# Local attention in four-bank units with the band mask multiplied in by VectorE, and the last head pair of each global attention normalized through TensorE and ScalarE

## The chip, the cores and the metric

The kernel runs on one core of one Trainium2 chip. The metric is the device time of one execution in microseconds (us). Engine names are those of the profile: PE is TensorE (PEld its weight loads), DVE is VectorE, ACT is ScalarE, POOL is GpSimd, and SP issues transfers. Each engine works through its own list of instructions; the order in that list is fixed when the kernel is built, partly by the order in which the program emits them and partly by a scheduler that moves them.

## The reference, cut to what matters

```python
x = A_x                                             # (1, 2048, 512) bf16, 32 heads of 16
x = x + _A_ref(_layernorm(x), A_wqkv, A_wo)         # local: each query sees 8 keys, 0, 2, ... 14 back
x = x + _B_ref(_layernorm(x), B_wq, B_wk, B_wv, B_wo)   # global: 2048 keys, one shared K and V head
x = x + _A_ref(_layernorm(x), A_wqkv, A_wo)
x = x + _B_ref(_layernorm(x), B_wq, B_wk, B_wv, B_wo)
```

So four stages run one after the other, A0, B0, A1 and B1. A later stage needs the whole result of the one before, with a LayerNorm between.

## The kernel before

The sequence is cut into four chunks `c` of 512 rows (even and odd positions lie in different chunks, so a dilated window of 8 becomes a dense band). A chunk is projected (`a_in`), attended (`a_attn`), projected out (`a_out`), and its LayerNorm and projections for the B stage follow (`b_in`). `a_attn` goes over four head groups `t` of 8 heads; the texts call one such `t` a head pair. The part that the argument touches:

```python
for t in range(4):                                 # a_attn(c), before
    o, dn = ...                                    # two PSUM banks: outputs, softmax sums
    for gh in range(2):
        for kd in range(2):                        # a unit: two row groups, two PSUM banks
            st = self.sps.tile([128, 2, 512], F32, name="s")            # sps has 2 buffers
            for j in range(2):                     # band mask (0 or -30000) added by PE
                nc.tensor.matmul(st[:, j, 0:ncol], lhsT=self.w.ident[:], rhs=self.w.band[:, 0:ncol],
                                 start=True, stop=False)
            ...                                    # 8 score matmuls on top of the mask
            nc.scalar.activation(out=P[:, :, 0:ncol], in_=st[:, :, 0:ncol], func=AF.Exp, scale=DH ** -0.5)
            ...                                    # 16 PV matmuls into o, 4 sum matmuls into dn
    nc.scalar.activation(out=logs[:], in_=dn[:], func=AF.Ln)
    nc.scalar.activation(out=rec[:], in_=logs[:], func=AF.Exp, scale=-1.0)     # 1 / sums
    nc.vector.tensor_tensor(out=onc[:, t, :], in0=o[:], in1=rec[:], op=ALU.mult)
    self.checks.see_logs(logs[:], tmp[:])          # a guard: POOL adds up logs*logs
...
def run(self, plan0):                              # order of a whole A stage
    self.a_in(0, plan0)
    self.a_in(1, plan)
    for c in range(4):
        self.a_attn(c)
        if c + 2 < 4:
            self.a_in(c + 2, plan)
        self.a_out(c)
        self.b_in(c, plan)
```

In `a_in` the keys were copied out of PSUM and then masked twice by POOL. At the end of B, the last head pair was normalized like every other: its sums went by DMA to a reciprocal, on to DRAM and back as a broadcast, and only then could the last output projection run.

Of the kernel before, what the change touches and what calls it, by code (L numbers as in the profile page):

```python
# [428 lines left out]
class Checks:  # L429
# [7 lines left out]
    def __init__(self, nc, pool):  # L437
        self.nc, self.pool = nc, pool
        self.a = pool.tile([128, 512], F32, name="chk_a")
        self.b = pool.tile([128, 2, 32], F32, name="chk_b")  # L440
        nc.gpsimd.memset(self.a[:], 0.0)
        nc.gpsimd.memset(self.b[:], 0.0)

    def see_logs(self, logs, tmp):

        self.nc.gpsimd.tensor_tensor(out=tmp, in0=logs, in1=logs, op=ALU.mult)  # L446
        self.nc.gpsimd.tensor_tensor(out=self.a[:], in0=self.a[:], in1=tmp, op=ALU.add)
# [6 lines left out]
    def flag(self, psum_pool):  # L454
        nc, pool = self.nc, self.pool
        ok = pool.tile([128, 512 + 64], F32, name="chk_ok")
        for out, in_, lim in ((ok[:, 0:512], self.a[:], self.LOG_A ** 2), (ok[:, 512:544], self.b[:, 0, :], self.SUM_B),
                              (ok[:, 544:576], self.b[:, 1, :], self.REC_B)):
            nc.vector.tensor_scalar(out=out, in0=in_, scalar1=lim, scalar2=None, op0=ALU.is_lt)
        mn = pool.tile([128, 1], F32, name="chk_mn")  # L460
        nc.vector.tensor_reduce(out=mn[:], in_=ok[:], axis=AX.X, op=ALU.min)
        mb = pool.tile([128, 2], BF16, name="chk_mb")
        nc.vector.tensor_copy(out=mb[:, 0:1], in_=mn[:])
        nc.vector.memset(mb[:, 1:2], 1.0)
        cnt = psum_pool.tile([1, 1], F32, name="chk_cnt")
        nc.tensor.matmul(cnt[:], lhsT=mb[:, 0:1], rhs=mb[:, 1:2], start=True, stop=True)
        bad = pool.tile([1, 1], mybir.dt.int32, name="chk_bad")
        nc.vector.tensor_scalar(out=bad[:], in0=cnt[:], scalar1=127.5, scalar2=None, op0=ALU.is_lt)
        return bad
# [50 lines left out]
def build_band_mask(nc, cpool):  # L520
# [3 lines left out]
    nc.gpsimd.memset(m[:], 0.0)  # L524
    for h in range(2):
        for n in range(5):
            w = NQ if n < 4 else SPILL
            ap = m[64 * h:64 * h + 64, n * NQ:n * NQ + w]
            b = 0 if n < 4 else 64
            nc.gpsimd.affine_select(out=ap, in_=ap, compare_op=ALU.is_ge, fill=-30000.0, base=b, pattern=[[1, w]],  # L530
                                    channel_multiplier=-1)
            nc.gpsimd.affine_select(out=ap, in_=ap, compare_op=ALU.is_ge, fill=-30000.0, base=7 - b,  # L532
                                    pattern=[[-1, w]], channel_multiplier=1)
    return m
# [12 lines left out]
class Phase:  # L547
# [3 lines left out]
    def __init__(self, ctx, tc, x_sb, x_bf, w, QT, KAB, VE, checks, tag):  # L551
# [5 lines left out]
        self.sps = pool("As", 2, space=PSUM)  # L557
        self.ops = pool("Ao", 1, space=PSUM)
        self.mps = pool("Am", 2, space=PSUM)
        self.sm = pool("Asm", 2)  # L560
        self.xnp = pool("Axn", 4)
        self.xtp = pool("Axt", 2)
        self.qp = pool("Aq", 2)
        self.kp = pool("Ak", 3)
        self.ktp = pool("Akt", 3)
        self.pp = pool("Ap", 4)
        self.oncp = pool("Aonc", 2)
        self.np = pool("An", 2)
        self.checks = checks
        vp = pool("Av", 1)  # L570
        self.vbuf = [vp.tile([128, 8, 4, 2, 2, 32], BF16, name=f"V{i}") for i in range(3)]
        self.nhalf = vp.tile([128, 4], F32, name="nhalf")
        nc.gpsimd.memset(self.nhalf[:], -0.5)
# [3 lines left out]
        self.n = 0  # L577

    def copy(self, out, in_, act=None):

        if act is None:
            self.n += 1
            act = self.n % 2 == 0
        if act:
# [3 lines left out]
    def ln_T(self, src, plan):  # L588
# [6 lines left out]
        for i in range(4):  # L595
            nc.vector.bn_stats(out=stats[:, i, :], in_=src(i))
            nc.vector.bn_aggr(out=mv[:, i, :], in_=stats[:, i, :])
        nc.vector.tensor_scalar_add(out=ve[:], in0=mv[:, :, 1], scalar1=EPS)
        nc.gpsimd.tensor_tensor(out=rstd[:], in0=ve[:], in1=self.nhalf[:], op=ALU.pow)
# [24 lines left out]
    def a_in(self, c, plan):  # L624
# [6 lines left out]
        for t in range(4):  # L631
# [3 lines left out]
            kt_ = self.ktp.tile([128, 512], BF16, name="kt")  # L635
            self.copy(kt_[:], ps[:])
            for a in range(2):
                nc.gpsimd.tensor_scalar(out=k[:, t, :, a, :], in0=kt_[:].rearrange("p (b i) -> p b i", i=64), scalar1=self.w.kmask[:, a:a + 1], scalar2=None,  # L638
                                        op0=ALU.mult)
        v = self.vbuf[c % 3]  # L640
        wv = w_sb[:, :, 2 * D:].rearrange("p k (r a d) -> p k a r d", a=2, d=DH)
        for k2 in range(4):
# [8 lines left out]
            for gh in range(2):  # L651
                dst = v[:, 2 * k2:2 * k2 + 2, :, gh, :, 16 * gh:16 * gh + DH].rearrange("p b t j d -> p (b t) j d")
                self.copy(dst, ps[:].rearrange("p b (t h j) d -> p (b t) h j d", h=2, j=2)[:, :, gh, :, :])

    def a_attn(self, c):
# [4 lines left out]
        for t in range(4):  # L660
# [9 lines left out]
            for gh in range(2):  # L670
                for kd in range(2):
                    spill = kd == 0 and c % 2 == 1
                    ncol = 4 * NQ + (SPILL if spill else 0)
                    parts = []
                    for i in range(4):
                        kb = 4 * kd + i
                        parts.append((i * NQ, NQ if kb < 7 else 64, k, v, kb, 64 * kb))
                    if spill:
                        parts.append((4 * NQ, SPILL, kprev, vprev, 7, 0))
                    st = self.sps.tile([128, 2, 512], F32, name="s")  # L680
                    for j in range(2):
                        nc.tensor.matmul(st[:, j, 0:ncol], lhsT=self.w.ident[:], rhs=self.w.band[:, 0:ncol],  # L682
                                         start=True, stop=False)
                    for n, (col, w, kk, vv, kb, q0) in enumerate(parts):
                        for j in range(2):
                            g = 2 * gh + j
                            gs = slice(32 * g, 32 * g + 32)
                            nc.tensor.matmul(st[:, j, col:col + w], lhsT=kk[gs, t, kb, :, :],  # L688
                                             rhs=q[gs, t, q0:q0 + w], start=False, stop=(n == len(parts) - 1),
                                             tile_position=(32 * g, 0))  # L690
                    P = self.pp.tile([128, 2, 4 * NQ + SPILL], BF16, name="P")
                    nc.scalar.activation(out=P[:, :, 0:ncol], in_=st[:, :, 0:ncol], func=AF.Exp, scale=DH ** -0.5)  # L692
                    for n, (col, w, kk, vv, kb, q0) in enumerate(parts):
                        for j in range(2):
                            for a in range(2):
                                r = 2 * j + a
                                nc.tensor.matmul(o[32 * r:32 * r + 32, q0:q0 + w],
                                                 lhsT=vv[64 * a:64 * a + 64, kb, t, gh, j, :],
                                                 rhs=P[64 * a:64 * a + 64, j, col:col + w], start=first("o", r),
                                                 stop=False, skip_group_check=True, tile_position=(64 * a, 32 * r))  # L700
                    for j in range(2):
                        js = slice(64 * j, 64 * j + 64)
                        nxt = 4 if kd == 0 else 3
                        pj = P[:, j, 0:4 * NQ].rearrange("p (b q) -> p b q", q=NQ)
                        dj = dn[js, :].rearrange("p (b q) -> p b q", q=64)
                        jobs = [(dj[:, 4 * kd:4 * kd + 4, :], pj[:, :, 0:64]),
                                (dj[:, 4 * kd + 1:4 * kd + 1 + nxt, 0:SPILL], pj[:, 0:nxt, 64:NQ])]
                        if spill:
                            jobs.append((dj[:, 0, 0:SPILL], P[:, j, 4 * NQ:4 * NQ + SPILL]))
                        for out, rhs in jobs:  # L710
                            nc.tensor.matmul(out, lhsT=self.w.halves[:, gh, :], rhs=rhs, start=first("d", j), stop=False,  # L711
                                             skip_group_check=True, tile_position=(0, 64 * j))
            logs = self.np.tile([128, 512], F32, name="logs")
            rec = self.np.tile([128, 512], F32, name="rec")
            tmp = self.np.tile([128, 512], F32, name="tmp")
# [3 lines left out]
            self.checks.see_logs(logs[:], tmp[:])  # L719

    def a_out(self, c):
        nc = self.nc
        onc = self.onc.pop(c)
        for qi in range(4):
# [6 lines left out]
            nc.vector.tensor_tensor(out=self.x_sb[:, tt, :], in0=old[:, tt, :], in1=y[:], op=ALU.add)  # L731

    def b_in(self, c, plan):
# [14 lines left out]
        cols = self.VE[:, 4 * c:4 * c + 4, :, :]  # L748
        nc.gpsimd.memset(cols[:, :, :, 17:32], 0.0)
        for j in range(NJ):  # L750
            nc.gpsimd.memset(cols[:, :, j, 16:17], J_W[j])
# [6 lines left out]
    def run(self, plan0):  # L758
        plan = ("g", "a", "g", "v")
        self.a_in(0, plan0)  # L760
        self.a_in(1, plan)
        for c in range(4):
            self.a_attn(c)
            if c + 2 < 4:
                self.a_in(c + 2, plan)
            self.a_out(c)
            self.b_in(c, plan)


def attn_B_fast(ctx, tc, QT, KAB, VE, wo_sb, x_sb, S, tag, checks, out_view=None, st_bufs=2, pv_lag=3, y_gap=2,  # L770
# [8 lines left out]
    opp = ctx.enter_context(tc.tile_pool(name=f"Bf_o_{tag}", bufs=1, space=PSUM))  # L779
# [314 lines left out]
```

## Time and profile before

| | before |
|---|---|
| time, median of 3 runs | 1860.32 us (1856.23 to 1863.41) |
| span of the profiled run | 1853.3 us |
| first B exponential of B0 | 209.3 us |
| last exponential of B0 to first of B1 (joint and A1) | 229.5 us |
| last exponential of B1 to the end | 30.5 us |

I cut the span where the stages change: first transpose of A, last PV matmul of A, first and last exponential of B. The first fence is the table of busy time by stretches for the kernel before. The columns are: stretch, its length, then busy microseconds (and instruction count) of PE, PEld, DVE, ACT and POOL, then the granted PE clock as a share of full speed, the DMA share and GB/s. The lines are A0's attention, A0's tail, B0, the joint, A1's attention, A1's tail, and the end.

```profile
13.60:187.30 173.70, 158.91 (x2677) 93.03 (x2697) 68.05 (x152) 90.08 (x162) 100.02 (x80) 0.96 0.04 10
187.30:209.30 22.00, 13.40 (x85) 5.99 (x79) 9.87 (x21) 5.11 (x10) 5.13 (x5) 0.77 0.00 0
209.30:900.60 691.30, 565.83 (x5628) 190.45 (x5642) 668.87 (x1079) 687.42 (x513) 31.34 (x45) 0.99 0.05 11
900.60:934.00 33.40, 9.70 (x62) 3.29 (x60) 21.44 (x45) 3.05 (x4) 5.41 (x26) 0.71 0.05 13
934.00:1107.00 173.00, 158.39 (x2672) 92.32 (x2694) 65.30 (x137) 89.96 (x162) 99.01 (x79) 0.95 0.01 2
1107.00:1130.10 23.10, 14.57 (x85) 6.17 (x86) 10.30 (x22) 5.10 (x10) 5.12 (x5) 0.63 0.00 1
...
1822.80:1853.30 30.50, 9.82 (x58) 3.28 (x55) 8.76 (x17) 2.16 (x2) 1.77 (x3) 0.67 0.12 34
```

The B stage is bound by ACT (687 of 691 us). In A's attention PE is busy 159 of 174 us while DVE and ACT stand at 68 and 90. The change rests on the conclusion that PE bounds the stage, and that work moved from PE to DVE is won. The joint and the end are gaps in which every engine is mostly idle.

The next fence shows the groups of instructions of A that the change touches, from the page of the kernel before. A line gives the source line, the engine, the operation, the names, the shapes and the count; then busy us and the mean ns of one; then the idle time before and what ended it.

```profile
L692 ACT ACTIVATE P<-s 128x576 bf16<-128x576 f32 (+1 forms) x128 | 78.9, 650 | 50.4 <-PE s L688 50.2
L638 POOL TENSOR_SCALAR k<-kt,kmask 128x512 bf16<-128x512 bf16 x64 | 99.0, 1566 | 6.0 <-ACT kt L585 6.0
L682 PE MATMUL s<-bandmask,ident 128*128 128x288 bf16 (+1 forms) x256 | 58.5, 297 | 7.4 <-POOL bandmask L532 5.8
L711 PE MATMUL dn<-P,halves 128*64 128x256 bf16 (+3 forms) x576 | 44.7, 232 | 9.5 <-ACT P L692 9.5
```

The mask costs 58.5 us of PE over both stages, and ACT waits 50 us for scores.

The joint before, from the timeline of 899 to 938 us (start, duration, engine, line, operation, names; in brackets the idle time before it and what ended it):

```profile
906.45 0.68 DVE L854 COPY X_13953<-o_ps 128x512 f32<-128x512 f32 x1
...
914.21 3.63 SPq L510 DMA_DIRECT2D lb<-rd  x8
...
919.39 1.26 POOL L512 TENSOR_TENSOR onc<-X,lb 128x512 bf16<-128x512 f32 x1 [7.60 <-DMA lb<-rd]
...
925.86 0.69 DVE L879 TENSOR_TENSOR x_sb<-x_sb,dv 128x512 f32<-128x512 f32 x1 [0.41 <-PE dv L868]
...
926.93 1.76 DVE L575 MEMSET V_14061<- 128x2048 uint32 x1 [0.38 <-issue]
...
937.08 1.46 PE L621 MATMUL ps<-xnT,w_sb 128*128 128x512 bf16 x3 [0.82 <-DVE xnT L586]
```

Thirteen microseconds pass between the copy of the last sums and their use, nearly all of it in chained transfers, and three memsets of 1.76 us then stand ahead of the LayerNorm.

### The profile page before, as it was taken

The numbers are of one execution on the slowest core, as the hardware profiler recorded it, in microseconds if no ns is written. First come the engines' busy times: TensorE is split into PE (matmuls) and PEld (weight loads), VectorE is DVE, ScalarE is ACT, GpSimd is POOL, SyncE is SP. The second block draws the span as 40 slices with busy tenths as digits, with TensorE's granted clock in tenths as the row PEclk, the third lists the DMA queues.
The fourth block names the chain that finished last, engine by engine and source line by source line (L and its number), as shares of the span: only waits on it lengthen the run. The fifth ranks groups of instructions, "written<-read, shape, count | busy, mean of one in ns | idle before, by whom it ended". The sixth has DMA issues, their size and how long they took to land. (4 is left out here: it accounts for less than half of the span.)

```text
span 1853.3 us, 41000 instructions
## 1 busy us (share of the span) xinstructions
PE 1493.1 (81%) x16864; PEld 586.6 (32%) x16929; DVE 1533.1 (83%) x2568; ACT 1573.2 (85%) x1371; POOL 285.9 (15%) x354
## 2 busy tenths in 40 slices
PE   6998777778877888888589987777888788878884
PEld 4554222222222222222145542222222222222221
DVE  5432599999999999999744336999999999999995
ACT  3555599999999999999445456999999999999993
POOL 8653100000000000000076530000000000000000
PEclk9999799999999999999889997999999999999997
DMA  3000000000000000000000000000000000100000
GB/s 115 2 2 2 1 11 11 11 11 10 11 11 10 11 11 13 11 14 13 10 1 3 2 2 1 10 11 11 10 11 22 11 11 11 25 12 15 23 10 23
DMA packets 42675, 23.75 MB, mean 13 GB/s; under 512 B 30192, under 2 KB 35824, under 8 KB 42480
## 3 DMA queue, kind: packets, MB, share of 16 engines
q1 hardware_dynamic: 41904, 19.48, 4.6%
q8 instruction: 134, 2.20, 0.5%
q10 hardware_dynamic: 576, 1.57, 0.2%
q14 instruction: 61, 0.50, 0.1%
HBM read 13.66 MB, written 2.62 MB: 9 GB/s over the span
## 5 line engine op out<-in xcount | busy, mean ns | idle before, releaser
L817 ACT ACTIVATE pt<-st 128x1536 bf16<-128x1536 f32 x1024 | 1379.7, 1760 | 8.4 <-PE dv L811 5.4
L823 DVE TENSOR_SCALAR tt<-dv 128x512 int16<-128x512 f32 x1024 | 702.9, 686 | 42.6 <-PE dv L811 4.3
L828 DVE TENSOR_SCALAR it<-tt 128x2048 int16<-128x2048 int16 x1024 | 712.8, 697 | 0.0
L811 PE MATMUL st<-QT,KAB 32*128 32x512 bf16 x3072 | 409.9, 385 | 203.3 <-ACT pt L817 190.0
L836 PE MATMUL o_ps<-it,VE 128*32 128x512 bf16 x4096 | 442.0, 387 | 16.9 <-DVE it L828 15.9
L836 PE MATMUL o_ps<-pt,VE 128*32 128x512 bf16 x3072 | 409.8, 391 | 5.6 <-DVE X L854 1.8
L811 PE MATMUL dv<-QT,KAB 32*128 32x512 bf16 x1024 | 390.3, 381 | 26.3 <-DVE tt L823 18.7
L836 PEld LDWEIGHTS <-VE 128*32 128x32 bf16 x7168 | 211.2, 93 | 510.9 <-issue 475.9
L811 PEld LDWEIGHTS <-KAB 32*128 32x128 bf16 x4096 | 163.8, 91 | 479.2 <-issue 459.9
L692 ACT ACTIVATE P<-s 128x576 bf16<-128x576 f32 (+1 forms) x128 | 78.9, 650 | 50.4 <-PE s L688 50.2
L718 DVE TENSOR_TENSOR onc<-o,rec 128x512 bf16<-128x512 f32 x32 | 22.1, 691 | 98.7 <-ACT rec L717 98.7
L638 POOL TENSOR_SCALAR k<-kt,kmask 128x512 bf16<-128x512 bf16 x64 | 99.0, 1566 | 6.0 <-ACT kt L585 6.0
L512 POOL TENSOR_TENSOR onc<-X,lb 128x512 bf16<-128x512 f32 x32 | 44.4, 1388 | 233.7 <-DMA lb<-rd 211.9
L682 PE MATMUL s<-bandmask,ident 128*128 128x288 bf16 (+1 forms) x256 | 58.5, 297 | 7.4 <-POOL bandmask L532 5.8
L621 PE MATMUL ps<-xnT,w_sb 128*128 128x512 bf16 x244 | 62.1, 400 | 2.5 <-DVE xnT L586 0.8
L606 ACT ACTIVATE xn<-x_sb,nmr,rstd 128x512 bf16<-128x512 f32 x13 | 10.5, 812 | 52.7 <-DVE nmr L600 52.7
L586 DVE CAST q<-ps 128x512 bf16<-128x512 f32 x32 | 22.1, 691 | 40.0 <-PE ps L621 35.7
L614 PE MATMUL pT<-ident,xn 128*128 128x128 bf16 x256 | 27.4, 249 | 34.2 <-POOL xn L610 17.8
L585 ACT CAST kt<-ps 128x512 bf16<-128x512 f32 x32 | 18.7, 585 | 40.4 <-PE ps L621 40.4
L868 PE MATMUL o_ps<-woB_sb,onc 128*128 128x512 bf16 x87 | 29.9, 407 | 28.2 <-POOL onc L512 12.7
L711 PE MATMUL dn<-P,halves 128*64 128x256 bf16 (+3 forms) x576 | 44.7, 232 | 9.5 <-ACT P L692 9.5
L446 POOL TENSOR_TENSOR tmp<-logs 128x512 f32<-128x512 f32 x32 | 33.3, 1040 | 114.2 <-ACT logs L716 114.2
(235 smaller groups left out, 854.5 us busy)
## 6 DMA issues: line engine op xcount, KB each, us to landing
lb<-rd SPq DMA_DIRECT2D x256, 32.0 KB, 1.8
out_dram<-xo SPq DMA_DIRECT2D x4, 512.0 KB, 3.2
w_sb<-in_A_wqkv_dram ACTq DMA_DIRECT2D x4, 384.0 KB, 5.5
x_bf<-in_A_x_dram SPq DMA_DIRECT2D x3, 512.0 KB, 9.4
x_bf<-in_A_x_dram SPq DMA_DIRECT2D x2, 256.0 KB, 5.1
woA<-in_A_wo_dram SPq DMA_DIRECT2D x8, 64.0 KB, 5.2
wq_sb<-in_B_wq_dram SPq DMA_DIRECT2D x4, 128.0 KB, 2.2
woB_sb<-in_B_wo_dram SPq DMA_DIRECT2D x4, 128.0 KB, 2.6
```

The costliest lines, as they stand in the source:

```text
L446: self.nc.gpsimd.tensor_tensor(out=tmp, in0=logs, in1=logs, op=ALU.mult)
L512: nc.gpsimd.tensor_tensor(out=out, in0=X[:], in1=lb[:], op=ALU.mult)
L621: self.nc.tensor.matmul(ps[:], lhsT=wcols(kt), rhs=xnT[:, kt, :], start=(kt == 0), stop=(kt == 3))
L638: nc.gpsimd.tensor_scalar(out=k[:, t, :, a, :], in0=kt_[:].rearrange("p (b i) -> p b i", i=64), scalar1=self.w.kmask[:, a:a + 1], scalar2= ...
L682: nc.tensor.matmul(st[:, j, 0:ncol], lhsT=self.w.ident[:], rhs=self.w.band[:, 0:ncol], start=True, stop=False)
L692: nc.scalar.activation(out=P[:, :, 0:ncol], in_=st[:, :, 0:ncol], func=AF.Exp, scale=DH ** -0.5)
L711: nc.tensor.matmul(out, lhsT=self.w.halves[:, gh, :], rhs=rhs, start=first("d", j), stop=False, skip_group_check=True, tile_position=(0, 6 ...
L811: chain("pe", nc.tensor.matmul(out, lhsT=KAB[32 * g:32 * g + 32, a, kt * 128:(kt + 1) * 128], rhs=QT[32 * g:32 * g + 32, t, qc * 512:(qc + ...
L817: nc.scalar.activation(out=pt[:], in_=st_tiles.pop(s)[:], func=AF.Exp, scale=scale)
L823: chain("dve", nc.vector.tensor_scalar(out=t_tiles[m][:, r, :], in0=dv_tiles.pop(s)[:], scalar1=T_SCALE, scalar2=T_BIAS, op0=ALU.mult, op1 ...
L828: chain("dve", nc.vector.tensor_scalar(out=it[:].bitcast(I16), in0=t_tiles[m][:], scalar1=0.25, scalar2=127.0 * 128.0 + J_OFF[j], op0=ALU. ...
L836: chain("pe", nc.tensor.matmul(o_ps[b][32 * g:32 * g + 32, :], lhsT=VE[:, kt, j, :], rhs=rhs, start=(b, g) not in started, stop=stop, tile ...
```

## The change

The intent is to relieve PE in A and to shorten the two gaps. In A: units of four row groups in four PSUM banks, so one exponential and one multiply where there were two exponentials; the band mask (now 0 or 1) is multiplied into the exponentials by DVE, and PE's mask matmuls go; keys are masked on their way out of PSUM by ACT and DVE instead of POOL; evacuations are balanced by a running load; and all four B projections are emitted behind the last attention, where each used to follow the attention of its own chunk. At the end of each B: the last head pair's sums come from a matmul with a selecting matrix, the reciprocal from Ln and Exp on ACT, and the output projection is started before they are ready. The memory of the B stage is set aside once for the whole kernel, so twelve of the sixteen LayerNorm statistics of A1 can be computed inside B0.

```diff
-        self.sps = pool("As", 2, space=PSUM)
+        self.sps = pool("As", 1, space=PSUM)
...
-            kt_ = self.ktp.tile([128, 512], BF16, name="kt")
-            self.copy(kt_[:], ps[:])
-            for a in range(2):
-                nc.gpsimd.tensor_scalar(out=k[:, t, :, a, :], in0=kt_..., scalar1=self.w.kmask[:, a:a + 1], ...)
+            nc.scalar.activation(out=k[:, t, :, 0, :], in_=pk, func=AF.Identity, scale=self.w.kmask[:, 0:1])
+            nc.vector.tensor_scalar(out=k[:, t, :, 1, :], in0=pk, scalar1=self.w.kmask[:, 1:2], ...)
...
-                    st = self.sps.tile([128, 2, 512], F32, name="s")
-                    for j in range(2):
-                        nc.tensor.matmul(st[:, j, 0:ncol], lhsT=self.w.ident[:], rhs=self.w.band[:, 0:ncol], ...)
+                st = self.sps.tile([128, 4, 512], F32, name="s")
...              # 16 score matmuls
+                nc.scalar.activation(out=P[:, :, 0:ncol], in_=st[:, :, 0:ncol], func=AF.Exp, scale=DH ** -0.5)
+                nc.vector.tensor_tensor(out=P[:, :, 0:ncol], in0=P[:, :, 0:ncol],
+                                        in1=self.w.band[:, 0:ncol].unsqueeze(1).to_broadcast([128, 4, ncol]),
+                                        op=ALU.mult)
...              # 32 PV matmuls, then 8 sum matmuls with the column halves adjacent
-            self.checks.see_logs(logs[:], tmp[:])
+            self.checks.see_logs(logs[:])
...              # memory for QT, KAB, VE and the order of the pools: left out here
+        self.a_in(0, quick); self.a_in(1, slow)          # one call a line in the original
+        self.a_attn(0); self.a_in(2, slow)
+        self.a_attn(1); self.a_in(3, slow); self.a_out(0)
+        self.a_attn(2); self.a_out(1)
+        self.a_attn(3)
+        self.b_in(0, slow); self.b_in(1, slow); self.a_out(2)
+        self.b_in(2, slow); self.a_out(3); self.b_in(3, quick)
...              # last head pair of a B
+        dn = opp.tile([128, 512], F32, name="o_ps")
+        chain("pe", nc.tensor.matmul(dn[:], lhsT=w.sel[:], rhs=X[:], start=True, stop=True))
+        nc.scalar.activation(out=logs[:], in_=dn[:], func=AF.Ln)
+        nc.scalar.activation(out=rec[:], in_=logs[:], func=AF.Exp, scale=-1.0)
+            chain("dve", nc.vector.tensor_tensor(out=onb[b][:], in0=X[:], in1=rec[:], op=ALU.mult))
```

## The prediction

> **What bounds it now.** The busy tenths and the table by stretches show four stages: local attention A (0 to 209 us), global attention B (to 902), A (first PE work 934, to 1130), B, plus a tail to 1853. In B, ACT is 99.7% busy (1.345 us per step, 512 steps): B is ACT-bound with DVE at 97.5%. In A, PE is busy 173 of 211 us and no vector engine over 55%: A is PE plus latency. Each A takes 196 us from its first transpose to its first B exponential.
>
> **A: what changes, from the timeline.** One head pair t takes 5.45 us with projections mixed in. PE start-to-start in it: the two band-mask matmuls of a unit 0.35 us, 8 scores 0.24, 16 PV 0.24, 4 denominator matmuls 0.24, four units: 4.3 us. Removed: masks, 1.4 us per t. Denominators are reordered so the two column halves are adjacent; V projections already run such pairs (256 columns, 0.061 us each instead of 0.107), so I count 0.7 instead of 0.96. New PE work about 2.6 us per t: 27 us less over 16 t.
> Added: DVE multiplies 128x1152 bf16, two per t. The Trainium skill ("VectorE: DVE Perf Modes", Mode 2x_1P) gives two elements a cycle at 0.96 GHz, so 0.66 us, an estimate no record of this trace tests. 21 us of DVE per A. Exponentials: 32 of about 1.13 us instead of 64 of 0.65 (estimate from 0.65 at 576 columns). Key masking leaves POOL (8 x 1.57 us per chunk) for one ACT (0.69) and one DVE (0.75) pass.
> New waits: scores have one four-bank buffer, so scores(n+1) waits for exp(n): about 1.9 us per unit, 4.5 us per t with logs, where little filler is left. Also the new order leaves b_in(1), out(2), b_in(2), out(3), b_in(3) serial after the last attention: about 44 us, two LayerNorm chains of 5 to 7 us each with PE idle and then at half clock (0.43 instead of 0.23 us per 512-column matmul; skill, "TensorE: Matmul & The Clock Gate", Part 1: 427 and 216 ns; the trace agrees), against 19 us before. Sum: 13.6 start + about 130 + 44 = 187 instead of 209. I take -21 per A.
>
> **Joint B to A.** Before: last exp ends 902.4, DMA normalization to 919, add at 926.5, then three memsets (1.76 us each) hold LayerNorm: first projection 937. After: statistics are computed inside B (12 x 0.8 us on DVE, absorbed), denominators by one fp32 matmul (about 1 us), Ln, Exp (0.6 each), multiply, four matmuls, V memsets between: first projection about 915. -21 us.
>
> **End.** Same replacement; but in DVE order the checks and a 1600-wide reduce (about 1.8 us, from 0.75 at 576) stand between the output adds. Last DMA about 1837 instead of 1848 in old time: -10.
>
> **B interior.** Ln/Exp and waits of the second last block, statistics: +3.
>
> Sum: -21-21-21-10+3 = -70: 1790 us, range 1764 to 1818. Faster 0.93, same 0.06, slower 0.01.
>
> **What would show it.** First B exponential near 187; A1's first projection 12 to 15 us after B0's last exponential; multiply near 0.66 us; B steps still 1.345; idle PE in the last 40 us of A; end tail 19 us after last exponential.
>
> **What would make it wrong.** The multiply at one element per cycle (1.2 us) or the single score buffer serializing ACT and PE: A at 200 or more. Serial tail longer than 44. DVE statistics stalling ACT in B. Or attention packing better than 4.5 us per t: A at 170.

## The result, and the profile after

The kernel after took 1827.62 us (median of 4 runs, 1825.62 to 1832.83), the kernel before 1860.15 us beside it. The ratio is 0.983 with a 95% interval of 0.980 to 0.986: 1.7% faster, so within 2%, where 3.8% had been predicted.

The same stretches for the kernel after (A0's attention, A0's tail, B0, joint, A1's attention, A1's tail, end):

```profile
14.00:161.70 147.70, 115.81 (x2440) 73.48 (x2460) 83.89 (x153) 87.59 (x131) 55.19 (x50) 0.90 0.05 12
161.70:211.70 50.00, 33.84 (x199) 15.28 (x192) 17.27 (x41) 17.55 (x34) 6.61 (x7) 0.75 0.00 1
211.70:906.00 694.30, 584.17 (x5632) 186.00 (x5642) 675.97 (x1108) 689.27 (x514) 38.38 (x50) 0.99 0.05 11
906.00:922.40 16.40, 9.09 (x63) 3.20 (x55) 14.60 (x22) 4.69 (x6) 2.98 (x2) 0.96 0.00 1
922.40:1063.30 140.90, 110.50 (x2436) 72.03 (x2459) 77.72 (x133) 86.61 (x130) 53.52 (x48) 0.91 0.01 2
1063.30:1113.00 49.70, 33.53 (x203) 15.26 (x196) 17.27 (x41) 17.57 (x34) 6.61 (x7) 0.75 0.00 1
...
1802.70:1824.30 21.60, 9.54 (x64) 3.37 (x61) 10.63 (x20) 3.31 (x4) 2.97 (x2) 0.79 0.08 28
```

The sums, as differences of the profiled spans against what was predicted:

| term | predicted | measured | how |
|---|---|---|---|
| A0, start to first B exponential | -21 | +2.4 | 209.3 to 211.7 |
| joint | -21 | -17.0 | 33.4 to 16.4 |
| A1, first transpose to first B exponential | -21 | -5.5 | 173.0 + 23.1 to 140.9 + 49.7 |
| B0 and B1 | +3 | 0.0 | +3.0 and -3.0 |
| end | -10 | -8.9 | 30.5 to 21.6 |
| sum | -70 | -29.0 | 1853.3 to 1824.3 |

The joint and the end came in. PE lost 43 us of busy time in A0's attention (158.9 to 115.8), but 20 of them only moved into the tail (13.4 to 33.8); over the whole of A0 it lost 22.7, where 27 had been planned. The attention became 26 us shorter and the tail behind it 28 us longer. PE now idles 32 of 147.7 us in the attention, and its clock fell from 0.96 to 0.90 there. By its busy time PE no longer bounds it.

The groups that stand in place of those shown for before, from the page of after:

```profile
L695 DVE TENSOR_TENSOR P<-P,bandmask 128x1152 bf16<-128x1152 bf16 (+1 forms) x64 | 59.8, 934 | 35.7 <-ACT P L694 35.4
L694 ACT ACTIVATE P<-s 128x1152 bf16<-128x1152 f32 (+1 forms) x64 | 71.8, 1122 | 14.1 <-PE s L689 14.0
L728 ACT ACTIVATE logs<-dn 128x512 f32<-128x512 f32 x32 | 19.2, 600 | 44.5 <-PE dn L724 44.2
L705 PE MATMUL o<-P,V 64*32 64x72 bf16 (+2 forms) x2176 | 34.0, 206 | 21.4 <-DVE P L695 17.9
L642 DVE TENSOR_SCALAR k<-ps,kmask 128x512 bf16<-128x512 f32 x32 | 24.0, 749 | 31.0 <-ACT k L641 30.6
```

ACT's long wait is no longer for scores (50 us before, 14 after) but for the sums, ahead of the logarithm (44 us; 20 before, in a group that the page leaves out); and PE now waits 18 us for the multiply, which did not exist before. The multiply takes 934 ns on average, where 660 had been reckoned.

How the chain runs is seen in the timeline of after, at the end of A0's attention. Here one `t` of the last chunk, from the timeline of 134 to 162 us (weight loads and bystanders left out):

```profile
149.73 1.14 ACT L694 ACTIVATE P<-s 128x1184 bf16<-128x1184 f32 x1
...
151.02 1.27 POOL L448 TENSOR_TENSOR chk_a<-chk_a,logs 128x512 f32<-128x512 f32 x1
151.06 1.85 DVE L695 TENSOR_TENSOR P<-P,bandmask 128x1184 bf16<-128x1184 bf16 x1
...
152.97 0.70 PE L705 MATMUL o<-P,V 64*32 64x72 bf16 x40 [1.39 <-DVE P L695]
152.98 0.73 DVE L695 TENSOR_TENSOR P<-P,bandmask 128x1120 bf16<-128x1120 bf16 x1
...
154.52 0.65 PE L705 MATMUL o<-P,V 64*32 64x72 bf16 x32
155.11 0.71 PE L724 MATMUL dn<-P,halves 128*64 128x256 bf16 x8
155.75 0.38 PE L689 MATMUL s<-q,k 32*128 32x72 bf16 x16
155.92 0.60 ACT L728 ACTIVATE logs<-dn 128x512 f32<-128x512 f32 x1 [2.13 <-PE dn L724]
...
156.41 1.15 ACT L694 ACTIVATE P<-s 128x1184 bf16<-128x1184 f32 x1
157.60 0.78 DVE L695 TENSOR_TENSOR P<-P,bandmask 128x1184 bf16<-128x1184 bf16 x1 [3.76 <-ACT P L694]
```

Exponential, multiply, PV and sums follow each other with the engines taking turns. ACT's next instruction is the logarithm, and it idles 2.1 us until the sums (155.11) have come. The next exponential stands behind the logarithm on ACT, and its last scores (155.75) behind the sums on PE; it starts at 156.41. From 149.73 to 156.41 is 6.7 us for one `t`; the prediction had 4.5, and 5.45 was measured before, with projections mixed in. The three periods of that chunk average 6.7 us in A0 and 5.8 in A1. Two multiplies of nearly equal size take 1.85 and 0.73 us. The slow one starts 0.04 us after POOL's add for the guard has started.

The joint after, from its timeline of 904 to 926 us:

```profile
910.10 1.76 DVE L579 MEMSET V<- 128x2048 uint32 x1 [0.63 <-PE o_ps L856]
...
911.78 0.63 DVE L890 COPY X<-o_ps 128x512 f32<-128x512 f32 x1
912.47 1.12 PE L894 MATMUL o_ps<-X,sel 128*128 128x512 f32 x2 [1.36 <-DVE X L890]
...
914.97 0.69 DVE L902 TENSOR_TENSOR onb<-X,lb 128x512 bf16<-128x512 f32 x1 [0.42 <-ACT lb L898]
...
916.04 1.76 DVE L579 MEMSET V<- 128x2048 uint32 x1 [0.38 <-issue]
...
921.09 1.27 DVE L940 TENSOR_TENSOR x_sb<-x_sb,st 128x512 f32<-128x512 f32 x2
...
925.42 1.01 PE L626 MATMUL ps<-xnT,w_sb 128*128 128x512 bf16 x2 [0.67 <-ACT xnT L589]
```

Copy to normalized rows takes 3.2 us now, not 13. The first projection comes 17.5 us after the end of the last exponential (907.9), where 34.3 were taken before (937.1 less 902.8) and 12 to 15 predicted. Two of the three memsets still hold DVE: one at 910.10 ahead of the copy of the sums, one at 916.04 ahead of the adds.

### The profile page after: what moved, and what is told of

It is laid out like the page before. It is cut to its first block, busy times and chain, and to the rows that moved or that the text cites. A ratio compares the mean times of both kernels' runs of the same rounds, so it can differ in the third digit from the quotient of the medians.

```text
span 1824.3 us, 40411 instructions
## 1 busy us (share of the span) xinstructions
PE 1459.2 (80%) x16615; PEld 560.3 (31%) x16689; DVE 1577.7 (86%) x2612; ACT 1596.9 (88%) x1363; POOL 209.7 (11%) x256
## 4 chain that ended last, share of the span: by engine, by line
ACT 37%; DVE 30%; PE 15%; issue 14%; DMA 1%; SPq 1%; POOL 1%; DVEq 0%; ACTq 0%; POOLq 0%
ACT pt L837 33%; DVE tt L843 11%; DVE it L848 11%; PE ps L626 5%; PE o_ps L856 2%; PE st L831 2%; DVE P L695 2%; ACT P L694 1%; DVE X L876 1%; DVE stats L601 1%; PE pv L654 1%; DVE x_sb L745 1%; PE dv L831 1%; PE dn L724 1%; PE o L705 1%
## 5 line engine op out<-in xcount | busy, mean ns | idle before, releaser
L453 POOL TENSOR_TENSOR chk_b<-chk_b,S 128x32 f32<-128x32 f32 x30 | 11.8, 395 | 1030.5 <-DMA S<-X 895.8
L695 DVE TENSOR_TENSOR P<-P,bandmask 128x1152 bf16<-128x1152 bf16 (+1 forms) x64 | 59.8, 934 | 35.7 <-ACT P L694 35.4
L694 ACT ACTIVATE P<-s 128x1152 bf16<-128x1152 f32 (+1 forms) x64 | 71.8, 1122 | 14.1 <-PE s L689 14.0
L626 PE MATMUL ps<-xnT,w_sb 128*128 128x512 bf16 x231 | 67.2, 419 | 13.6 <-ACT q L589 5.0
L728 ACT ACTIVATE logs<-dn 128x512 f32<-128x512 f32 x32 | 19.2, 600 | 44.5 <-PE dn L724 44.2
L705 PE MATMUL o<-P,V 64*32 64x72 bf16 (+2 forms) x2176 | 34.0, 206 | 21.4 <-DVE P L695 17.9
L642 DVE TENSOR_SCALAR k<-ps,kmask 128x512 bf16<-128x512 f32 x32 | 24.0, 749 | 31.0 <-ACT k L641 30.6
L447 POOL TENSOR_TENSOR logs<-logs 128x512 f32<-128x512 f32 x32 | 34.6, 1080 | 128.6 <-ACT rec L729 128.6
L448 POOL TENSOR_TENSOR chk_a<-chk_a,logs 128x512 f32<-128x512 f32 x32 | 45.7, 1430 | 2.5
L626 PE MATMUL ps<-xnT,wq_sb 128*128 128x512 bf16 x122 | 37.6, 452 | 4.7 <-ACT QT L589 4.0
```

The lines of the kernel that those rows point to most:

```text
L447: self.nc.gpsimd.tensor_tensor(out=logs, in0=logs, in1=logs, op=ALU.mult)
L448: self.nc.gpsimd.tensor_tensor(out=self.a[:], in0=self.a[:], in1=logs, op=ALU.add)
L626: self.nc.tensor.matmul(ps[:], lhsT=wcols(kt), rhs=xnT[:, kt, :], start=(kt == 0), stop=(kt == 3))
L695: nc.vector.tensor_tensor(out=P[:, :, 0:ncol], in0=P[:, :, 0:ncol], in1=self.w.band[:, 0:ncol].unsqueeze(1).to_broadcast([128, 4, ncol]), ...
L705: nc.tensor.matmul(o[32 * r:32 * r + 32, q0:q0 + w], lhsT=vv[64 * a:64 * a + 64, kb, t, gh, j, :], rhs=P[64 * a:64 * a + 64, g, col:col + ...
```

## The experiments

Eleven kernels ran in three batches; each gave a correct result. "A0" is the time of the first B exponential, "middle" is last exponential of B0 to first of B1, both from the profiled run. Two limits hold for what follows. Two ratios whose intervals overlap may not differ at all; that is said where it matters. And the stage times come from one profiled run of each kernel: B0, whose code is the same in the twelve kernels other than before, took 692 to 697 us in them, so a few us in one stage of one trace are not read as an effect.

| kernel | median us | ratio to before, 95% interval | A0: attention + tail | A0 | middle | end |
|---|---|---|---|---|---|---|
| before | 1857 to 1860 | 1 | 173.7 + 22.0 | 209.3 | 229.5 | 30.5 |
| after | 1827.62 | 0.983 [0.980, 0.986] | 147.7 + 50.0 | 211.7 | 207.0 | 21.6 |
| e1_old_local | 1832.11 | 0.986 [0.983, 0.988] | 172.1 + 23.8 | 209.9 | 214.2 | 21.6 |
| e2_old_order | 1847.37 | 0.994 [0.992, 0.997] | 179.7 + 23.5 | 217.2 | 218.7 | 21.5 |
| e3_no_watch | 1816.60 | 0.977 [0.973, 0.980] | 143.3 + 50.2 | 207.3 | 206.1 | 22.1 |
| e4_ahead | 1809.86 | 0.974 [0.972, 0.977] | 134.7 + 54.4 | 203.1 | 197.7 | 21.6 |
| e5_dummy | 1855.22 | 0.999 [0.996, 1.002] | 164.9 + 43.1 | 222.2 | 223.6 | 21.7 |
| e6_two_bank | 1839.72 | 0.992 [0.989, 0.995] | 143.4 + 51.9 | 209.3 | 213.8 | 23.5 |
| e7_pe_mask | 1824.58 | 0.982 [0.980, 0.985] | 150.9 + 41.2 | 206.6 | 208.5 | 21.0 |
| e8_ahead_order | 1799.70 | 0.969 [0.965, 0.973] | 132.3 + 47.9 | 194.0 | 197.1 | 21.7 |
| e9_ahead_mask | 1801.91 | 0.970 [0.968, 0.973] | 131.3 + 49.8 | 194.9 | 194.8 | 23.0 |
| e10_ahead_nowatch | 1793.45 | 0.965 [0.962, 0.967] | 128.4 + 47.4 | 189.6 | 194.7 | 21.7 |
| e11_late_ln | 1826.19 | 0.983 [0.980, 0.985] | 144.3 + 49.7 | 207.8 | 211.9 | 21.7 |

### e1_old_local: the old A stage with the new joint and end

```diff
-        self.sps = pool("As", 1, space=PSUM)
+        self.sps = pool("As", 2, space=PSUM)
-                st = self.sps.tile([128, 4, 512], F32, name="s")
+                    st = self.sps.tile([128, 2, 512], F32, name="s")
+                    for j in range(2):
+                        nc.tensor.matmul(st[:, j, 0:ncol], lhsT=self.w.ident[:], rhs=self.w.band[:, 0:ncol], ...)
...   # old a_in, copy(), a_attn and order of the stages; new end of B kept
```

> The kernel after, but local attention (units of two banks, mask on PE, key masking on POOL, order of stages) as before; the new end of each B and the hoisted memory stay. Theory: the new local attention is worth nothing, all gain is at the joint and the end: 1826 us, within 6 of the kernel after, first B exponential near 209. Rival: the new local attention is worth the 10 to 20 us per stage that was forecast and something else lost it: 1840 or more.

It took 1832.11 us, 4 to 5 us more than after in the median. So the joint and the end carry 25 us of the change's gain (1857.6 before in that batch, 1832.1 here), and the whole rebuilt local attention is worth about 4.5 us, not 42. The intervals of the two ratios overlap, so even that is not clear of zero; 42 us would be 0.023 in the ratio, and the two differ by 0.003. In the profiled runs A0 is even 1.8 us longer after than here, and the middle 7 us shorter.

### e2_old_order: the new attention in the old order of the stages

```diff
-        self.a_attn(3)
-        self.b_in(0, slow)
-        self.b_in(1, slow)
...
+        for c in range(4):
+            self.a_attn(c)
+            if c + 2 < 4:
+                self.a_in(c + 2, slow)
+            self.a_out(c)
+            self.b_in(c, quick if c == 3 else slow)
```

> The kernel after with the old order of stages (a_attn, a_in, a_out, b_in per chunk), units of four groups kept. Theory (the serial tail behind the last attention, 49 us instead of 22, costs most of the gain): the tail falls to about 22 us, the attention before it grows by less than that, first B exponential at about 195 instead of 212, total about 1795. Rival (PE work is what bounds, so moving it changes nothing): first B exponential within 4 us of 212.

The tail came back to 23.5 us, as the theory behind this run had it, but the attention grew by 32 us, and the kernel became 20 us slower. The theory that the long tail is what ate the gain fell: the tail's work only moved. With the old order A is 5.5 us longer in A0 and 11.7 us in the middle, so the new order was a gain, and the waits are inside the attention. Beside e1_old_local, which has the old attention in this same order, it is 15 us slower (ratios 0.994 and 0.986, intervals apart, same batch): the new attention, with its key masking and evacuations, is by itself a loss, and the new order makes up for it.

### e3_no_watch: the guard on the logarithms taken away

The result stays right; only the guard's input is missing, so this is no kernel to ship.

```diff
-            self.checks.see_logs(logs[:])
```

> The kernel after without the two POOL operations per head pair that watch the logarithms (the safety check sees zeros; the result stays right). Theory (the adds on POOL slow the DVE multiplies that they overlap, 1.0 to 1.85 us instead of 0.75, and those sit on the chain): every multiply 0.72 to 0.80 us, 4 to 6 us less per local stage, total about 1817. Rival (slow multiplies are hidden): less than 2 us in all.

This gave 11 us in the median. The four runs spread from 1811 to 1823 us, and the profiled one is the slowest: in it A0 is 4.4 us shorter than in after and the middle 0.9, so the size is uncertain. In after, 20 of the 64 multiplies took over 0.9 us, against a normal 0.76; the excess adds up to 11.3 us. Without the guard 3 did, with an excess of 0.9 us, and the mean fell from 934 to 775 ns, as its page shows:

```profile
L695 DVE TENSOR_TENSOR P<-P,bandmask 128x1152 bf16<-128x1152 bf16 (+1 forms) x64 | 49.6, 775 | 35.9 <-ACT P L694 35.6
```

That the lost excess is on the path in full is not shown. The Trainium skill explains the slow ones ("SBUF — State Buffer", section "Who interferes with whom"): a DVE instruction with two SBUF inputs contends with a GpSimd instruction that reads SBUF, and whichever comes second blocks until the first is done. The trace agrees closely. For the 17 slow multiplies that began while one of the guard's two instructions was running, the duration is the rest of POOL's instruction plus 0.60 us, within 0.04 us each time. Shown above: POOL's add ends at 151.02 + 1.27 = 152.29, which is 1.23 us after the multiply's start at 151.06; 1.23 + 0.60 = 1.83, and 1.85 was recorded. The other three slow ones began behind POOL's normalized rows. Where the multiply began first, POOL's add took 1.65 to 1.78 us instead of 1.27 (12 adds).

### e4_ahead: the next unit issued ahead of this unit's PV

Scores, exponential and multiply of unit n+1 are emitted before the PV and sum matmuls of unit n, also across the border between two `t`; the logarithm thereby falls behind the next `t`'s first exponential.

```diff
+        units = [(t, kd) for t in range(4) for kd in range(2)]
+        head(*units[0])                       # scores, exponential, multiply
+        for n, (t, kd) in enumerate(units):
+            if n + 1 < len(units):
+                head(*units[n + 1])
+            body(t, kd)                       # PV and sums
+            if kd == 1:
+                finish(t)                     # logarithm, reciprocal, multiply, guard
```

> The kernel after with the scores and the exponential of the next unit issued ahead of the PV products of this one, so that the logarithm no longer stands between. Theory (a head pair is a serial chain exp, exp, multiply, PV, sums, log of about 6.2 us late in the stage): 4.5 us per head pair there, the last PV 10 to 15 us earlier, but fewer projections fit into the gaps and move behind it; net 5 to 10 us per stage, total about 1812. Rival (ACT or PE throughput bounds a head pair): period unchanged within 0.3 us.

This gave 18 us with the same work on every engine. PE's busy time is the same (114.9 us in A0's attention), the stretch 13 us shorter. From the lists of waits over the attention of A0 (engine, line, releaser: us in total, times, longest), first after, then e4_ahead:

```profile
ACT logs L728 <- PE dn L724: 21.2, 12, 3.1
...
PE o L705 <- DVE P L695: 9.4, 13, 1.6
...
ACT P L694 <- PE s L689: 7.7, 7, 3.9
```

```profile
ACT P L691 <- PE s L686: 12.1, 13, 2.8
...
ACT logs L735 <- PE dn L728: 9.2, 7, 3.0
```

ACT's waits for the sums fell from 21.2 to 9.2 us, while those for the scores rose from 7.7 to 12.1. One `t` in the last chunk takes 5.0 us on average instead of 6.7. So the serial chain, not the amount of work, set the pace.

### e5_dummy and e7_pe_mask: the mask's matmuls added, and exchanged for the multiply

e5_dummy issues four matmuls of the mask's size into each unit's scores, which the scores then overwrite; it was to keep PE's clock up. e7_pe_mask is the same but the matmuls add the real mask and the multiply is gone.

```diff
+                for g in range(4):
+                    nc.tensor.matmul(st[:, g, 0:ncol], lhsT=self.w.ident[:], rhs=self.w.band[:, 0:ncol],
+                                     start=True, stop=True)           # e5; stop=False in e7
...
-                nc.vector.tensor_tensor(out=P[:, :, 0:ncol], in0=P[:, :, 0:ncol], in1=...,   # e7 alone
-                                        op=ALU.mult)
```

> The kernel after, with four dummy matmuls (the size of the removed mask) written to the score buffer ahead of each unit's scores and overwritten by them. Theory (half of the missing gain is PE at a lower granted clock, because it now waits more): the granted clock of the attention part rises from 0.90 to 0.95 or more and the 0.5 us per unit that the dummies cost is mostly paid back: first B exponential within 6 us of 212. Rival (the chain of latencies alone sets the pace, the clock is a bystander): 32 times 0.4 to 0.5 us are added, first B exponential at 225 to 228.

> The kernel after with units of four groups, but the mask added on PE as before and no DVE multiply. Theory (the multiply of 0.75 to 1.85 us is longer on the chain than the mask matmuls of about 0.5 us that it replaced, and it lowers PE's clock): attention part shorter by 5 to 12 us, clock 0.95, total about 1812. Rival (PE work bounds the stage): 22 us per stage longer, total about 1870.

The attention of A0 in the two, first e5_dummy, then e7_pe_mask:

```profile
13.90:178.80 164.90, 134.49 (x2545) 82.55 (x2566) 82.34 (x154) 90.29 (x135) 54.59 (x50) 0.93 0.04 11
```

```profile
14.00:165.00 151.00, 127.49 (x2566) 78.29 (x2589) 57.91 (x124) 90.36 (x135) 50.88 (x50) 0.99 0.04 12
```

The dummies cost 28 us. The theory that a higher clock pays them back fell: A0 ended at 222.2, not within 6 us of 212. It fell a little short of the rival's 225 too, and the clock rose only from 0.90 to 0.93, so the run does not show that the clock is a bystander. What it shows is that four mask matmuls in a unit lie on the chain. Over both A stages with their tails (A0 10.5 us, middle 16.6) they cost 27.1 / 64 units = 0.42 us per unit. Taking the multiply away from e5_dummy (which gives e7_pe_mask's instructions) saves 31 us in all: A0 15.6 and middle 15.1, or 0.48 us per unit. The two costs cancel: e7_pe_mask is within 3 us of after, with overlapping intervals, and both its theory (1812) and its rival (1870) fell. Moving the mask from PE to DVE has taken a piece off the chain and put one of the same size on it. How much of the multiply's cost is PE's lower clock (0.90 in after, 0.99 in e7_pe_mask) was not separated.

### e6_two_bank: units of two row groups with the multiply on DVE

```diff
-        self.sps = pool("As", 1, space=PSUM)
-        self.pp = pool("Ap", 2)
+        self.sps = pool("As", 2, space=PSUM)
+        self.pp = pool("Ap", 4)
-            for kd in range(2):
+            for gh in range(2):
+                for kd in range(2):
-                st = self.sps.tile([128, 4, 512], F32, name="s")
+                    st = self.sps.tile([128, 2, 512], F32, name="s")
```

> The kernel after with units of two row groups, two score buffers of two banks and four P buffers as before; mask still multiplied on DVE. Theory (one four-bank score buffer makes a head pair serial): with two buffers the next scores run under the exponential, the attention part shortens by 8 to 15 us, total about 1808. Rival (unit size does not matter, ACT's order with the logarithm does): within 4 us per stage of the kernel after.

Two score buffers and smaller units made it 12 us slower than after, 2.4 us better in A0 and 7 us worse in the middle. So the gain that the theory put on a second score buffer did not come. The run changes the size of the units as well (twice as many exponentials and multiplies), so it does not show that a second buffer by itself is worth nothing.

### e8_ahead_order: e4_ahead, and the tail's work in another order

```diff
         self.b_in(0, slow)
-        self.b_in(1, slow)
         self.a_out(2)
+        self.b_in(1, slow)
         self.b_in(2, slow)
```

> The run with scores issued ahead (e4_ahead), and the output projection of chunk 2 issued before the inputs of B for chunk 1. Theory (each LayerNorm chain in the tail leaves PE idle 5 to 7 us): one of the two chains is covered by the projections of chunk 1, tail 54 to about 47 us, total about 1796. Rival (tail is bound by PE and the evacuations): tail within 2 us of 54.

1799.70 us, 10 us below e4_ahead and 28 us below after. With the output of chunk 2 placed early, the tail of A0 fell from 54.4 to 47.9 us: the LayerNorm of chunk 2 can run under projections of chunk 1, and PE's idle time before the transposes of the tail fell from 11.3 to 7.2 us. In A1 the tail fell too, from 52.3 to 47.4, but the attention before it took 4.3 us longer, and the middle gained only 0.6. This kernel is faster than both the kernel before (by 3.1%) and the kernel after, with a right result and all guards.

### e9_ahead_mask: e8_ahead_order with the mask back on PE

The edit is the one of e7_pe_mask, on e8_ahead_order.

> e8_ahead_order (next unit issued ahead, outputs of chunks moved between the projections) with the multiply taken away and the band mask added by PE (four 128-row matmuls per unit) again. In the changed kernel as it stands, the same swap (e7_pe_mask) cost nothing, because the chain scores-exponential-multiply-sums set the pace. Theory: once the next unit is issued ahead, PE's work sets the pace, so the mask's matmuls (about 128 of 0.23 us, 29 us per stage by the first measurement of their cost) come back on the path: attention of each stage about 145 us or more instead of 132 to 133, total above 1812. Rival: the multiply (0.78 us per unit behind each exponential, slowed by POOL) is still as dear as the mask's matmuls: total within 6 us of e8_ahead_order's 1800.

1801.91 us, within 2.2 us of e8_ahead_order: my theory fell, the rival held. The stretches show how. First e8_ahead_order, then e9_ahead_mask, A0's attention:

```profile
13.80:146.10 132.30, 108.19 (x2402) 68.58 (x2421) 80.95 (x150) 85.67 (x125) 57.07 (x50) 0.95 0.06 13
```

```profile
13.80:145.10 131.30, 115.85 (x2521) 73.20 (x2536) 53.73 (x115) 84.22 (x123) 49.97 (x50) 1.00 0.05 13
```

PE is only 7.7 us busier with the mask than without, where the mask cost 29 us of PE per stage in the kernel before, and the clock is 1.00 instead of 0.95. That the full clock is what pays for the rest was not tested by itself. Even in the better order, moving the mask from PE to DVE is worth nothing. That does not make PE free: in e5_dummy, work added to it cost 28 us.

### e10_ahead_nowatch: e8_ahead_order without the guard

> e8_ahead_order without the watch of the logarithms (two adds on POOL per head pair; the result is right all the same, only the guard is gone, so this is no kernel to ship). The changed kernel gained 11 us from this alone (e3_no_watch). Theory that the gain came from the multiply being on the serial chain: with the chain broken the watch costs little, 0 to 4 us, total 1796 to 1800. Rival, that POOL's time itself (the normalized rows behind the watch) holds the stage: again about 10 us, total near 1790.

1793.45 us, 6 us below e8_ahead_order: between theory and rival, but the intervals of the two overlap. Of the slow multiplies 4 are left instead of 14 (excess 0.9 us instead of 8.4). In the profiled runs A0 is 4.4 us shorter and the middle 2.4, about what e3_no_watch showed (4.4 and 0.9). So the lock seems to cost a few us still; whether it costs less than in after is not shown. A0 ends at 189.6 us, 2.6 us from the 187 of the prediction: with the chain opened, the tail reordered and the lock gone, the predicted stage is nearly there.

### e11_late_ln: only the logarithm late

```diff
+        for n, (t, kd) in enumerate(units):
+            head(t, kd)
+            if kd == 0 and t > 0:
+                finish(t - 1)
+            body(t, kd)
+        finish(3)
```

> The changed kernel with one half of e4_ahead alone: the logarithm and reciprocal of a head pair are issued behind the next pair's first exponential and multiply, but the scores of every unit stay behind the sums of the unit before on PE. Theory S: what e4_ahead gained (18 us) came from the scores issued ahead; then this alone gains little, 0 to 5 us (total 1822 to 1828), or loses some, as the next pair's outputs now wait for the two banks that the late logarithm still reads. Rival L: the logarithm standing in ScalarE's queue ahead of the next exponential was the hold-up; then this gains most of the 18 us, total 1808 to 1814.

1826.19 us, 1.4 us below after with overlapping intervals: theory S. So the late logarithm alone is not what e4_ahead gained by; the scores issued ahead are needed. Whether they would do it alone was not run. The `t` shown above speaks for needing both: there the last scores end at 155.75 + 0.38 = 156.13 and the logarithm at 156.52, so moving only one of the two would start the next exponential at most 0.4 us earlier, an estimate from this one `t`. In the list of waits over A0's attention in e11_late_ln, ACT's wait for the sums stays nearly as it was in after (21.2 us):

```profile
ACT logs L735 <- PE dn L728: 19.0, 12, 3.0
```

## Why the prediction was right or wrong

**Right: the joint and the end.** "-21 us" and "-10" were measured as -17.0 and -8.9. Replacing the chained transfers by a matmul, Ln and Exp did what was reckoned: from the copy of the sums to the normalized rows it takes 3.2 us instead of 13, which is about 10 of the 17 us at the joint. The other 7 came elsewhere (statistics computed inside B, the output projection started early) and were not split. The missing 4 us are probably the two V memsets of 1.76 us in the way, which I knew of ("V memsets between") and set too low; no run took them away, and DVE's normalized rows and statistics stand between the adds as well. e1_old_local shows that these two terms alone are nearly the whole gain of the change.

**Right in that it is small: the B interior.** "+3" and "B steps still 1.345": B0 +3.0, B1 -3.0 us, together 0, and 1.35 to 1.36 us per step in both kernels. A term of 3 us is within what B0 varies by between the profiled runs (692 to 697 us after the change), so its number is not confirmed.

**Wrong: local attention.** The step that failed is "Sum: 13.6 start + about 130 + 44 = 187 instead of 209. I take -21 per A." A0 ended at 211.7, and the two A stages together gained 3 us, not 42. That is 39 of the 41 us by which the sum missed; the joint and the end missed by 5 the same way, and B by 3 the other way. In A0 the attention is 18 us over its 130 and the tail 6 over its 44. Its terms:

- *"about 1.9 us per unit, 4.5 us per t with logs"* was the term most in error. The attention took 147.7 and 140.9 us instead of 130, and one `t` of A0's last chunk 6.7 us. The prediction does not show how its 130 follows from the 4.5. It named the single score buffer as a risk; e4_ahead keeps that buffer. I had listed the links of the chain but summed them as if only scores and exponential waited for each other. In the trace the chain also runs through multiply, PV and sums, because the next `t`'s scores stand behind the sums on PE and its exponential behind the logarithm on ACT. Loosening both (e4_ahead) brought 18 us with no work removed; putting only the logarithm later (e11_late_ln) brought 1.4, which is within the noise.
- *"so 0.66 us, an estimate no record of this trace tests"*. An unhindered multiply took 0.72 to 0.78 us. The section I cited counts elements per cycle alone, which at 0.96 GHz would be an estimate of 0.60 us; the prediction does not say where its other 0.06 come from; the same page of the Trainium skill, "VectorE: DVE Perf Modes", section "The TRN2 errata — SBUF-src ops pay a fixed extra latency per instruction", gives a measured fixed term of about 150 cycles. From it follows an estimate of (1152 / 2 + 150) / 0.96 GHz = 0.76 us, which the trace confirms. On top of that came the lock between DVE and POOL, which I had not thought of: mean 934 ns. e3_no_watch puts it at 11 us in the medians and 5 us in the A stages of the profiled runs. The prediction feared a multiply at one element per cycle (1.2 us); the cause was another one.
- *"Removed: masks, 1.4 us per t."* PE did lose this work, and by e5_dummy it is worth 28 us to have it off PE. But e5_dummy, e7_pe_mask and e9_ahead_mask show that the multiply put in its place costs about as much. The prediction's sum counted the multiply as 21 us of DVE's time, and gave it no place on the path.
- *"serial after the last attention: about 44 us"* was seen in kind (idle PE in the last part, half clock) and came out at 50.0 and 49.7. Its clock was 0.75. The Trainium skill ("TensorE: Matmul & The Clock Gate", Part 1) has 427 and 216 ns for the two rates of a 512-column matmul; the trace has 0.43 and 0.22 us between them in this tail, so that part held. e8_ahead_order shows that the order of the tail's work was worth 6.5 us of e4_ahead's tail in A0 and 4.9 in A1.

**What stays open.** Issuing the scores ahead without the late logarithm was not run, and PE's granted clock was never varied by itself, so its share in the multiply's cost is not known. Why A0's attention is 6.8 us longer than A1's in the kernel after, when they were nearly equal before, was not pursued. e10_ahead_nowatch's gain was not split between multiply and normalized rows. And an allocation of the guard that never meets a multiply was not built.

## What to carry to other kernels

That an engine is busy 90% of a stage does not yet say what work moved off it will win; before you count such work as time won, write down the chain that one unit of work runs through and put the new instruction into it. Here, moving a cost to another engine that stands on the same chain won nothing, while issuing the next unit's first links ahead of this unit's last won 18 us without removing any work, against about 4.5, not clear of noise, for the whole rebuilt attention. Before giving DVE a two-input SBUF instruction, look for POOL work that reads SBUF beside it, even a guard that nobody waits for.

## What the Trainium skill lacked or had wrong

- "SBUF — State Buffer" ("Who interferes with whom") is right on the lock, but does not say what the blocked instruction costs once it is free. Seventeen blocked multiplies of 1120 to 1184 bf16 columns needed 0.60 us (within 0.04 us) after POOL's end, against 0.72 to 0.78 us when unhindered. That some of the fixed part passes while the instruction waits is a guess from these numbers.
- "VectorE: DVE Perf Modes": the section "Mode 2×_1P" gives the rate alone, and its example does not point to the fixed term, which the page has only in later sections; an estimate of 0.60 us by rate, 0.76 us measured for 1152 columns.
